# Top-k attention with a feed-forward block: small operations moved to ScalarE, and scores, value products, exponentials and sends placed elsewhere in the step

## The chip, the cores and the metric

The kernel runs on one core of one Trainium2 chip. The core has five engines that run side by side, each through its own instructions in the order in which they were written: PE (TensorE, matrix products), DVE (VectorE), ACT (ScalarE), POOL (GpSimd) and SP (SyncE, which here only issues DMAs). The metric is the device time of one execution in microseconds, as the median of several runs.

## The reference

Eight batches, eight heads, 576 positions, head width 64. Of each row of scores only the 32 largest take part in the softmax; the result feeds a layer norm, a hidden layer and a residual. The weights arrive as float64.

```python
scores = scale * np.matmul(q, k.transpose(0, 1, 3, 2))
kth = np.partition(scores, -32, axis=-1)[..., -32:-31]
scores = np.where(scores >= kth, scores, -1e9)
attn = np.exp(scores - scores.max(-1, keepdims=True))
attn = attn / (attn.sum(-1, keepdims=True) + 1e-9)
x = heads_to_columns(attn @ v)                      # (8, 576, 512)
xn = (x - mean(x)) / sqrt(var(x) + 1e-6) * g_ln
return x + maximum(xn @ w_ch1, 0) @ w_ch2           # 512 -> 2048 -> 512
```

## The kernel before

**Tiles.** Two heads form a pair. The 576 query rows of a pair are cut into four tiles of 128 rows and a rest of 64; a Unit is one such tile for both heads, so its scores are two tiles of 128 x 576. The rest units take the 64 rows of both heads as one tile. There are 160 units. Units are joined in Groups (the two or three query tiles of one Job, which is a batch and a pair), and a group's value products are made at once.

**What a unit goes through.** `scores` (L365) makes the scores on PE and copies them from PSUM with ACT (L371). `halve` (L399) splits a row on DVE into the larger and the smaller of two halves (L411, L412). `select` (L414), called four times, finds eight maxima each time and strikes them out, all on DVE (L425, L433, L419); the last one yields the 32nd value, `thr`, and the first one the maximum, `top`. `prepare` (L441) turns the maximum into the bias of the exponential with one tiny operation, on DVE in the first steps (below `CONVERTING`) and on POOL afterwards (L446). `watch` (L448) notes on DVE whether a second candidate of the smaller half could have been missed (L452). `mask` (L478, ACT) makes a steep ramp around the 32nd value, after one tiny multiplication (L482) for its bias; `lower` (L487, POOL, L488) subtracts the scores from it; `weigh` (L490, ACT, L496) takes the exponential and its sum. `move` (L519) transposes blocks of 32 x 32 on DVE (L524) from `e` into the unit's own score tile; SP then sends that tile to HBM (`send`, L540) and brings it back turned (`bring`, L532, four DMAs) as `pt`. Units that are not moved, the rest ones above all, are turned on PE instead (`turn`, L545). `values` (L606) multiplies `pt` with v on PE into `av`; `take_values` (L624) copies `av` to `oT` with ACT (L626); `place` (L636) turns `oT` on PE, and ACT writes it, divided by the sum, into the rows `x` (L630).

**The rows.** A Block is a pair of row tiles whose heads are all there. `stats` (L675) makes the mean and variance on DVE (L681, L682) and takes the mean off the rows with two POOL operations (L687, L690). `turn_x` turns the rows on PE (L715), then follow the hidden products (L756) and the projections (L913), which take seven eighths of the usual products through sums made on POOL (L843 to L849). This MLP work stands in a list, `todo`.

**The order.** Everything is written out by hand in one loop over steps (L1183). Step n runs `halve` and `select` of unit n, makes the scores of unit n + 1, masks unit n - 1 (`mk`), and weighs and moves unit n - 2 (`ex`); a group's value products come four steps behind its last unit. The step has eight calls of `fill` (L263), the slots. Each slot advances a clock (`tick`), runs what has become old enough (the classes `Later`: sends after `SEND_AGE` slots, brings `BRING_AGE` slots later), and puts as much MLP work on PE as `slot` (L1145) has planned for the step. So PE's list holds scores, value products, turns and MLP work in a fixed order, and ACT's list holds the copies that serve them between the masks and exponentials. While n is below `CONVERTING` (17), the float64 weights are also converted. `END` is the number of steps; the step at which a block's rows are taken is written at L1053. The second `compute` call (L1354) runs only if the watch finds a doubtful row.

The beginning of a step reads:

```python
for x in due(n):
    scores(x)
if g:
    values(g)
if u:
    halve(u)
    select(u, 0)
...
if ex and not early:
    weigh(ex, 0)
fill()
if ex and len(ex.tiles) > 1 and not early:
    weigh(ex, 1)
if g:
    take_values(g)
fill()
```

Of the kernel before, what the change touches and what calls it, by code (L numbers as in the profile page):

```python
# [9 lines left out]
AF = mybir.ActivationFunctionType  # L10
ALU = mybir.AluOpType
FP32 = mybir.dt.float32
# [7 lines left out]
STEEP = 2.0**90  # L20
# [9 lines left out]
def compute(  # L30
# [12 lines left out]
    nc = tc.nc  # L43
    P = nc.NUM_PARTITIONS
# [7 lines left out]
    scale = 1.0 / float(D) ** 0.5  # L52
# [9 lines left out]
    HALF = S // 2  # L62
# [123 lines left out]
    now = [-1]  # L186
# [71 lines left out]
                run()  # L258

    sums_later, ends_later, stores = Later(), Later(), Later()  # L260
    sends, brings, loads = Later(), Later(), Later()

    def fill(least=0):  # L263
        tick[0] += 1
        ends_later.settle(END_AGE)
        loads.settle(LOAD_AGE)
        brings.settle(BRING_AGE)
        sends.settle(SEND_AGE)
        fetch_forms(FETCH_AGE)
        owed[0] = min(owed[0] + share[0], 6.0)  # L270
        while todo and (not todo[0][3] or todo[0][3]()):
            if owed[0] < todo[0][1] / 2 and least <= 0:
                break
            least -= 1
            pop()
# [89 lines left out]
    def scores(u):  # L365

        u.sc = scpool.tile([P, 2, S], FP32, tag="sc", name="sc")
        made = [score_half(u, s) for s in range(2)]
        for t in range(len(u.tiles)):
            for s in range(2):  # L370
                nc.scalar.copy(  # L371
                    u.sc[:, t, s * HALF : (s + 1) * HALF], made[s][t][:, 0:HALF]
                )
# [64 lines left out]
            u.top = m  # L438
        u.thr = m

    def prepare(u):  # L441

        nt = len(u.tiles)
        u.bias, u.edge = u.thr[:, 0:nt, 5], u.thr[:, 0:nt, 6]
        eng = nc.vector if u.i < CONVERTING else nc.gpsimd
        eng.tensor_scalar(u.bias, u.top[:, 0:nt, 0], -scale, 0.0, ALU.mult, ALU.add)  # L446

    def watch(u):  # L448

        nt = len(u.tiles)  # L450
        c = 1 + 2 * (u.i % 16)
        nc.vector.tensor_tensor(  # L452
            watched[:, c : c + nt], u.hi[:, 0:nt, HALF + 7], u.thr[:, 0:nt, 7], ALU.subtract
        )
        if u.i % 16 == 15 or u.i == N - 1:
            u.ends_watch = True

    def settle_watch():

        for out, first, op in ((0, 0, ALU.max), (33, 1, ALU.min)):  # L460
# [17 lines left out]
    def mask(u, t):  # L478
        if u.e is None:
            u.e = epool.tile([P, 2, S], FP32, tag="e", name="e")  # L480
        if t == 0:
            nc.scalar.mul(u.edge, u.thr[:, 0 : len(u.tiles), 7], STEEP)  # L482
        nc.scalar.activation(  # L483
            u.e[:, t], u.sc[:, t], AF.Relu, bias=u.edge[:, t : t + 1], scale=-STEEP
        )

    def lower(u, t):  # L487
        nc.gpsimd.tensor_tensor(u.e[:, t], u.e[:, t], u.sc[:, t], ALU.subtract)  # L488

    def weigh(u, t):  # L490
        g = u.group
        if g.den is None:
            g.den = denpool.tile([P, 2 * J + 1], FP32, tag="den", name="den")
        col = 2 * u.qt + t
        u.weighed += 1
        nc.scalar.activation(  # L496
            u.e[:, t], u.e[:, t], AF.Exp, bias=u.bias[:, t : t + 1], scale=-scale,
            accum_out=g.den[:, col : col + 1],
        )
# [106 lines left out]
    def values(g):  # L606
        vb = g.job.v
        av = brief("av")
        for c in range(J):
            for h in range(2):  # L610
                nc.tensor.matmul(  # L611
                    av[h * D : (h + 1) * D, 0 : g.nq],
                    vb[:, h * J + c, :],
                    g.pt[:, 0 : g.nq // 32, 5 * h + c, :],
                    start=(c == 0),
                    stop=False,
                )
        nc.tensor.matmul(  # L618
            av[:, 0 : g.nq], g.job.ends[:], g.pt[:, 0 : g.nq // 32, J, :],
            start=False, stop=True,  # L620
        )
        g.av = av

    def take_values(g):  # L624
        g.oT = otpool.tile([P, GQ], FP32, tag="oT", name="oT")
        nc.scalar.copy(g.oT[:, 0 : g.nq], g.av[:, 0 : g.nq])  # L626
# [38 lines left out]
    class Block:  # L665
# [9 lines left out]
        def stats(self, i):  # L675
            x = self.x[i]
            if self.mv is None:
                self.mv = small.tile([P, J, 2], FP32, tag="mv", name="mv")
                self.rstd = small.tile([P, J], FP32, tag="rstd", name="rstd")
            st = brief_small.tile([P, 6], FP32, tag="st", name="st")  # L680
            nc.vector.bn_stats(out=st[:], in_=x)  # L681
            nc.vector.bn_aggr(out=self.mv[:, i, :], in_=st[:])  # L682
            if now[0] <= gives_first:
                nc.vector.tensor_scalar_sub(x, x, self.mv[:, i, 0:1])
            else:
                less = brief_small.tile([P, 1], FP32, tag="less", name="less")
                nc.gpsimd.tensor_scalar(  # L687
                    less[:], self.mv[:, i, 0:1], -1.0, 0.0, ALU.mult, ALU.add
                )
                nc.gpsimd.tensor_scalar(x, x, 1.0, less[:], ALU.mult, ALU.add)  # L690
            self.step[i] = now[0]

        def centred(self, i):
# [246 lines left out]

    PER_ROW = 1.71e-3
    SUM_AGE, END_AGE, FETCH_AGE, STORE_AGE = 7, 6, 10, 8
    SEND_AGE, BRING_AGE, LOAD_AGE = 2, 4, 4
    blocks = []
    plain_done, formed, used, fetched = [None], [None], [], [0]

# [65 lines left out]
    units = []  # L1012
# [5 lines left out]
            g.last = len(units) - 1  # L1018
        j.last = len(units) - 1
    N = len(units)  # L1020
    END = N + 7

    fresh = []
    for j in jobs:
# [25 lines left out]
    for j in jobs:  # L1050
        if j.hp == NHP - 1:
            b = j.b
            step = j.last + (3 if j.last < EARLY else 4 + units[j.last].moved)  # L1053
            tiles = [(b, qt) for g in j.groups for qt in g.qts if qt < J]
            dsts = [[(out[b, t[1] * P : (t[1] + 1) * P, :], full)] for t in tiles]
            if jobs.index(j) == NHP - 1:
                step -= 1
                j.groups[0].quick = True
            if tiles:
                add_block(step, tiles, dsts)  # L1060
            if J in j.groups[0].qts and b % 4 == 3:
# [17 lines left out]
    def at(i):  # L1079
        return units[i] if 0 <= i < N else None  # L1080
# [14 lines left out]
    def due(n):  # L1095

        return [units[n + 1]] if 0 < n < N - 1 else []
# [83 lines left out]
    for n in range(END):  # L1183
# [16 lines left out]
        last = ex and ex is ex.group.units[-1]  # L1200
        quick = ex.group if last and ex.group.quick else None

        for x in due(n):
            scores(x)
        if g:
            values(g)
        if u:
            halve(u)
            select(u, 0)
# [15 lines left out]
                weigh(ex, t)  # L1225
        if not quick:
            weights(n, 0)
        if ex and not early:
            weigh(ex, 0)
        fill()  # L1230
        if ex and len(ex.tiles) > 1 and not early:
            weigh(ex, 1)
        if g:
            take_values(g)
        fill()
        if parts:
            parts[0]()
        if ex and ex.rest:
# [6 lines left out]
        sums_later.settle(SUM_AGE)  # L1245
        for den in recips.pop(n, []):
            nc.vector.reciprocal(den, den)
        if doubt is not None and at(n - 1) and at(n - 1).ends_watch:
            settle_watch()
            if n == N:  # L1250
                tell()
        if n in turns:
            turn_heads(turns[n])
# [5 lines left out]
        fill()  # L1259
        if mk and not early:  # L1260
            mask(mk, 0)
        if g:
            place(g)
        if late:
            place_rest(late.job.b, late.job.hp)
        fill(1 if g or late else 0)
        if mk and len(mk.tiles) > 1 and not early:
            mask(mk, 1)
        fill()
        if mk and not early:  # L1270
            lower(mk, 0)
        if len(parts) > 2:
            parts[1]()
        if moved:
# [14 lines left out]
        fill()  # L1289
        if parts:  # L1290
            parts[-1]()
        if mk and len(mk.tiles) > 1 and not early:
            lower(mk, 1)
        fill()
        for x in (u if n < EARLY else None, mk if n > EARLY else None):
            if x and x is units[x.job.last]:
                load_values(x.job)
# [8 lines left out]
            weights(n, 1)  # L1306
        if u:
            select(u, 3)
            prepare(u)
        for x in (g, quick):  # L1310
            if x and x.job.hp == NHP - 1:
                for qt in x.qts:
# [73 lines left out]
```

## Time and profile before

| | us |
|---|---|
| median of three runs | 1741.08 (1738.31 to 1741.73) |
| the profiled execution | 1737.59 |
| its span, first to last instruction | 1735.7 |

| engine | busy us | share of the span |
|---|---|---|
| PE | 1485.2 | 86% |
| PE weight loads (beside the products) | 1110.8 | 64% |
| DVE | 1467.9 | 85% |
| ACT | 1032.2 | 59% |
| POOL | 1051.8 | 61% |

The 16 DMA engines move 275.19 MB, at a mean of 159 GB/s. The chain of work that ended last runs for 41% of the span on PE, 30% on DVE, 8% on ACT, 8% on DMAs and 7% on POOL. A busy share is a mean over stages with different limits; a wait is put down to what came last before the waiting instruction started. In the lines of the profile "out<-in" are the program's tile names, L is the line of the kernel, and the numbers after the bar are the group's busy time in us and the mean of one instruction in ns.

### The profile page before, as it was taken

The numbers are of one execution on the slowest core, as the hardware profiler recorded it, in microseconds if no ns is written. First come the engines' busy times: TensorE is split into PE (matmuls) and PEld (weight loads), VectorE is DVE, ScalarE is ACT, GpSimd is POOL, SyncE is SP. The second block draws the span as 40 slices with busy tenths as digits, with TensorE's granted clock in tenths as the row PEclk, the third lists the DMA queues.
The fourth block names the chain that finished last, engine by engine and source line by source line (L and its number), as shares of the span: only waits on it lengthen the run. The fifth ranks groups of instructions, "written<-read, shape, count | busy, mean of one in ns | idle before, by whom it ended". The sixth has DMA issues, their size and how long they took to land.

```text
span 1735.7 us, 26165 instructions
## 1 busy us (share of the span) xinstructions
PE 1485.2 (86%) x7412; PEld 1110.8 (64%) x7412; DVE 1467.9 (85%) x4090; ACT 1032.2 (59%) x2662; POOL 1051.8 (61%) x1321
## 2 busy tenths in 40 slices
PE   2558887887788888788899989999899899989997
PEld 1336455655566665566677766776677676768886
DVE  6979999989898998889998998899989998984100
ACT  6777765755566564556566756676566665644411
POOL 4668868646556564556656766576656665746334
PEclk9768898988999898899999999999999999989999
DMA  7525657744565465545775586556755676453411
GB/s 190 134 66 181 200 123 216 226 140 136 151 182 151 145 187 154 152 144 153 212 181 159 161 221 161 175 167 181 199 172 150 168 214 181 139 141 110 124 45 51
DMA packets 392068, 275.19 MB, mean 159 GB/s; under 512 B 254436, under 2 KB 358376, under 8 KB 391912
## 3 DMA queue, kind: packets, MB, share of 16 engines
q1 hardware_dynamic: 387176, 272.81, 55.8%
q8 instruction: 62, 1.02, 0.3%
q10 hardware_dynamic: 4736, 0.59, 0.2%
q14 instruction: 94, 0.77, 0.1%
HBM read 177.47 MB, written 95.81 MB: 157 GB/s over the span
## 4 chain that ended last, share of the span: by engine, by line
PE 41%; DVE 30%; ACT 8%; DMA 8%; POOL 7%; SPq 3%; issue 2%; DVEq 0%; ACTq 0%; POOLq 0%
PE ops L913 14%; PE hps L756 12%; DVE m L433 9%; DVE hi L419 7%; PE av L611 6%; DVE sc L524 5%; PE scps L390 4%; DMA pt<-turned 3%; POOL e L488 3%; DVE lo L412 3%; ACT e L496 2%; DVE hi L411 2%; DVE hi L425 2%; PE av L618 2%; SPq L532 2%
## 5 line engine op out<-in xcount | busy, mean ns | idle before, releaser
L488 POOL TENSOR_TENSOR e<-e,sc 128x576 f32<-128x576 f32 x288 | 424.0, 1482 | 295.8 <-ACT e L483 292.5
L756 PE MATMUL hps<-xT,w 128*128 128x256 f32 x2304 | 533.4, 384 | 3.2 <-ACT xT L718 3.2
L756 PEld LDWEIGHTS hps<-xT,w 128*128 128x128 f32 x2304 | 432.1, 192 | 74.3 <-issue 12.3
L433 DVE MAX8 m<-hi 128x8 f32<-128x296 f32 (+1 forms) x1152 | 469.9, 442 | 1.1
L419 DVE MATCH_REPLACE8 hi<-m,hi 128x288 f32<-128x288 f32 (+1 forms) x864 | 377.1, 441 | 0.0
L913 PE MATMUL ops<-w,h 128*128 128x256 f32 x1360 | 321.3, 385 | 0.0
L371 ACT COPY sc<-scps 128x288 f32<-128x288 f32 x576 | 202.7, 406 | 190.1 <-PE scps L390 167.2
L913 PEld LDWEIGHTS ops<-w,h 128*128 128x128 f32 x1360 | 256.2, 193 | 42.1 <-issue 7.5
L611 PE MATMUL av<-pt,vb 128*64 128x256 f32 (+2 forms) x1088 | 175.6, 473 | 101.4 <-DMA pt<-turned 62.7
L496 ACT ACTIVATE e<-e,m 128x576 f32<-128x576 f32 x288 | 224.9, 787 | 60.2 <-POOL e L488 59.9
L524 DVE STREAM_TRANSPOSE sc<-e 128x1152 f32<-128x1152 f32 x118 | 160.2, 1358 | 109.5 <-ACT e L496 103.0
L483 ACT ACTIVATE e<-sc,m 128x576 f32<-128x576 f32 x288 | 217.5, 774 | 5.2
L611 PEld LDWEIGHTS av<-pt,vb 128*64 128x64 f32 x1088 | 91.3, 161 | 174.4 <-issue 94.9
L446 POOL TENSOR_SCALAR m<-m 128x2 f32<-128x2 f32 (+1 forms) x143 | 109.3, 764 | 135.1 <-DVE m L433 132.0
L779 ACT ACTIVATE h<-hps 128x512 f32<-128x512 f32 x144 | 85.4, 594 | 102.3 <-PE hps L756 101.9
L412 DVE TENSOR_TENSOR lo<-sc 128x576 f32<-128x576 f32 (+1 forms) x160 | 144.2, 901 | 0.0
L390 PE MATMUL scps<-kT,qT 64*128 64x288 f32 x512 | 96.8, 480 | 46.0 <-DVE qT L320 40.6
L411 DVE TENSOR_TENSOR hi<-sc 128x576 f32<-128x576 f32 (+1 forms) x160 | 124.9, 780 | 6.6 <-ACT sc L371 6.4
L913 PE MATMUL ops<-wt,s 128*128 128x256 f32 x544 | 128.0, 383 | 0.0
L390 PE MATMUL scps<-kT,late_qT 64*128 64x288 f32 (+3 forms) x832 | 122.2, 412 | 2.1 <-ACT pt L565 2.1
L425 DVE MAX8 hi<-lo 128x8 f32<-128x288 f32 x288 | 117.8, 443 | 0.0
L913 PEld LDWEIGHTS ops<-wt,s 128*128 128x128 f32 x544 | 102.0, 192 | 16.6 <-issue 2.1
(104 smaller groups left out, 1664.4 us busy)
## 6 DMA issues: line engine op xcount, KB each, us to landing
turned<-sc SPq DMA_DIRECT2D x118, 576.0 KB, 3.3
pt<-turned SPq DMA_DIRECT2D x472, 144.0 KB, 3.0
w<-forms SPq DMA_DIRECT2D x136, 256.0 KB, 4.1
vb<-in_v_dram SPq DMA_DIRECT2D x136, 128.0 KB, 3.3
raw<-in_moe_w_ch_dram SPq DMA_DIRECT2D x32, 512.0 KB, 4.5
kT<-kept SPq DMA_DIRECT2D x36, 288.0 KB, 3.4
kin<-in_k_dram SPq DMA_DIRECT2D x128, 72.0 KB, 2.4
kept<-kT SPq DMA_DIRECT2D x32, 288.0 KB, 2.6
```

The lines of the kernel that those rows point to most:

```text
L371: nc.scalar.copy(u.sc[:, t, s * HALF : (s + 1) * HALF], made[s][t][:, 0:HALF])
L390: nc.tensor.matmul(ps[i * R : i * R + ql, o : o + width], qT[r, q0 : q0 + ql], kT[r, k0 : k0 + width], start=True, stop=True,)
L412: nc.vector.tensor_tensor(lo, a, b, ALU.min)
L419: nc.vector.match_replace(x, m[:, t, :], x, LOWEST)
L433: nc.vector.max(m[:, t, :], u.hi[:, t, 0:width])
L483: nc.scalar.activation(u.e[:, t], u.sc[:, t], AF.Relu, bias=u.edge[:, t : t + 1], scale=-STEEP)
L488: nc.gpsimd.tensor_tensor(u.e[:, t], u.e[:, t], u.sc[:, t], ALU.subtract)
L496: nc.scalar.activation(u.e[:, t], u.e[:, t], AF.Exp, bias=u.bias[:, t : t + 1], scale=-scale, accum_out=g.den[:, col : col + 1],)
L524: nc.vector.transpose(blocks.rearrange("p (j c n) -> p j c n", j=ni, n=32), u.e[:].rearrange("p t n -> p (t n)").rearrange("p (c j k) -> p ...
L611: nc.tensor.matmul(av[h * D : (h + 1) * D, 0 : g.nq], vb[:, h * J + c, :], g.pt[:, 0 : g.nq // 32, 5 * h + c, :], start=(c == 0), stop=False,)
L756: nc.tensor.matmul(ps[0][:, side * N : (side + 1) * N], w1[:, c, f * P : (f + 1) * P], self.xT[:, c, 0:N], start=(c == 0), stop=(c == NC - 1),
L913: nc.tensor.matmul(bank[name][:, 0:Q], a(j), rhs, start=first and j == 0, stop=(j == G - 1), skip_group_check=not first,)
```

## The change

It has these parts. The bias of the exponential is made by ACT in `mask`, between the masks of the unit's two tiles, and `prepare` is gone. `watch` uses, per tile, one operation with one tensor and a per-row number in place of one operation with two tensors for both tiles. Taking the mean off the rows goes from two POOL operations to two ACT operations, which are written two slots after the statistics (`CENTRE_AGE`). From step `CONVERTING` on, scores and value products are written behind the second slot, `take_values` behind the fifth and `place` at the end of the step, before the last slots. The exponential of a unit's first tile is written at the end of the step that masks it; the second stays after the first slot of the next step, which is now ahead of the scores. Sends wait four slots instead of two. Rows of a block that ends with a moved unit are taken one step later, the watch is settled one step later, and the loop has one more step.

```diff
+        centres.settle(CENTRE_AGE)
         brings.settle(BRING_AGE)
...
-    def prepare(u):
-        nt = len(u.tiles)
-        u.bias, u.edge = u.thr[:, 0:nt, 5], u.thr[:, 0:nt, 6]
-        eng = nc.vector if u.i < CONVERTING else nc.gpsimd
-        eng.tensor_scalar(u.bias, u.top[:, 0:nt, 0], -scale, 0.0, ALU.mult, ALU.add)
-    def watch(u):
-        nt = len(u.tiles)
-        c = 1 + 2 * (u.i % 16)
-        nc.vector.tensor_tensor(
-            watched[:, c : c + nt], u.hi[:, 0:nt, HALF + 7], u.thr[:, 0:nt, 7], ALU.subtract
-        )
...
         nc.scalar.activation(
             u.e[:, t], u.sc[:, t], AF.Relu, bias=u.edge[:, t : t + 1], scale=-STEEP
         )
+        if t == 0:
+            nc.scalar.mul(u.bias, u.top[:, 0:nt, 0], -scale)
+    def watch(u):
+        for t in range(len(u.tiles)):
+            c = 1 + 2 * (u.i % 16) + t
+            nc.vector.tensor_scalar(
+                watched[:, c : c + 1], u.hi[:, t, HALF + 7 : HALF + 8],
+                u.thr[:, t, 7:8], None, ALU.subtract,
+            )
...
-                less = brief_small.tile([P, 1], FP32, tag="less", name="less")
-                nc.gpsimd.tensor_scalar(
-                    less[:], self.mv[:, i, 0:1], -1.0, 0.0, ALU.mult, ALU.add
-                )
-                nc.gpsimd.tensor_scalar(x, x, 1.0, less[:], ALU.mult, ALU.add)
+                def centre():
+                    less = brief_small.tile([P, 1], FP32, tag="less", name="less")
+                    nc.scalar.mul(less[:], self.mv[:, i, 0:1], -1.0)
+                    nc.scalar.activation(x, x, AF.Identity, bias=less[:])
+                    self.step[i] = now[0]
+                centres.add(centre)
+                return
...
-    SEND_AGE, BRING_AGE, LOAD_AGE = 2, 4, 4
+    SEND_AGE, BRING_AGE, LOAD_AGE, CENTRE_AGE = 4, 4, 4, 2
...
-    END = N + 7
+    END = N + 8
...
-            step = j.last + (3 if j.last < EARLY else 4 + units[j.last].moved)
+            step = j.last + (3 if j.last < EARLY else 4 + 2 * units[j.last].moved)
...
-        for x in due(n):
-            scores(x)
-        if g:
-            values(g)
+        first = n < CONVERTING
+        if first:
+            for x in due(n):
+                scores(x)
+            if g:
+                values(g)
...
-        if ex and not early:
-            weigh(ex, 0)
         fill()
         if ex and len(ex.tiles) > 1 and not early:
             weigh(ex, 1)
-        if g:
+        if g and first:
             take_values(g)
         fill()
+        if not first:
+            for x in due(n):
+                scores(x)
+            if g:
+                values(g)
...
-        if g:
+        if g and first:
             place(g)
-        if late:
+        if late and first:
             place_rest(late.job.b, late.job.hp)
-        fill(1 if g or late else 0)
+        fill(1 if first and (g or late) else 0)
...
         if mk and not early:
             lower(mk, 0)
+        if g and not first:
+            take_values(g)
...
-        if mk and len(mk.tiles) > 1 and not early:
-            lower(mk, 1)
-        fill()
+        if mk and not early:
+            if len(mk.tiles) > 1:
+                lower(mk, 1)
+            weigh(mk, 0)
+        if not first:
+            if g:
+                place(g)
+            if late:
+                place_rest(late.job.b, late.job.hp)
+        fill(1 if not first and (g or late) else 0)
...
         if u:
             select(u, 3)
-            prepare(u)
```

More of the change, by code (lines that the diff above doesn't have):

```diff
@@ L260, in compute @@
     sums_later, ends_later, stores = Later(), Later(), Later()
-    sends, brings, loads = Later(), Later(), Later()
+    sends, brings, loads, centres = Later(), Later(), Later(), Later()
     def fill(least=0):
@@ L439, in select @@
         u.thr = m
-    def prepare(u):
-        nt = len(u.tiles)
-        u.bias, u.edge = u.thr[:, 0:nt, 5], u.thr[:, 0:nt, 6]
-        eng = nc.vector if u.i < CONVERTING else nc.gpsimd
-        eng.tensor_scalar(u.bias, u.top[:, 0:nt, 0], -scale, 0.0, ALU.mult, ALU.add)
-    def watch(u):
-        nt = len(u.tiles)
-        c = 1 + 2 * (u.i % 16)
-        nc.vector.tensor_tensor(
-            watched[:, c : c + nt], u.hi[:, 0:nt, HALF + 7], u.thr[:, 0:nt, 7], ALU.subtract
-        )
-        if u.i % 16 == 15 or u.i == N - 1:
-            u.ends_watch = True
     def settle_watch():
@@ L480, in mask @@
             u.e = epool.tile([P, 2, S], FP32, tag="e", name="e")
+        nt = len(u.tiles)
         if t == 0:
-            nc.scalar.mul(u.edge, u.thr[:, 0 : len(u.tiles), 7], STEEP)
+            u.bias, u.edge = u.thr[:, 0:nt, 5], u.thr[:, 0:nt, 6]
+            nc.scalar.mul(u.edge, u.thr[:, 0:nt, 7], STEEP)
         nc.scalar.activation(
@@ L485, in mask @@
         )
+        if t == 0:
[7 more added lines that the diff above has]
+            )
+        u.ends_watch = u.i % 16 == 15 or u.i == N - 1
     def lower(u, t):
@@ L1247, in compute @@
             nc.vector.reciprocal(den, den)
-        if doubt is not None and at(n - 1) and at(n - 1).ends_watch:
+        if doubt is not None and at(n - 2) and at(n - 2).ends_watch:
             settle_watch()
-            if n == N:
+            if n == N + 1:
                 tell()
```

## The prediction

> **What bounds the kernel now.** I read the utilisation row, then the windows by stage, then the list of waits, then one episode in the timeline. The windows give, per stretch: length, busy time of PE, PEld, DVE, ACT, POOL, then TensorE clock, DMA share and GB/s.
>
> ```profile
> 174.00:434.00 260.00, 210.34 (x1035) 140.51 (x1034) 248.93 (x679) 161.60 (x425) 178.13 (x192) 0.88 0.62 173
> 434.00:694.00 260.00, 219.46 (x1108) 162.72 (x1107) 238.00 (x659) 154.72 (x416) 146.79 (x186) 0.93 0.58 162
> 694.00:954.00 260.00, 229.14 (x1181) 173.45 (x1179) 237.47 (x665) 155.52 (x414) 157.45 (x210) 0.95 0.59 167
> 954.00:1214.00 260.00, 244.73 (x1270) 186.84 (x1272) 248.67 (x722) 168.34 (x445) 165.42 (x213) 0.97 0.64 178
> 1214.00:1474.00 260.00, 239.48 (x1251) 183.21 (x1247) 243.14 (x691) 160.90 (x425) 160.39 (x212) 0.97 0.64 180
> 1474.00:1600.00 126.00, 117.63 (x580) 93.25 (x579) 102.09 (x284) 68.98 (x180) 76.83 (x108) 0.96 0.46 135
> 1600.00:1736.00 136.00, 123.82 (x609) 106.14 (x607) 9.28 (x24) 34.45 (x79) 55.77 (x101) 0.97 0.24 72
> ```
>
> From 174 to 1600 us DVE is busy 1318.3 of 1426 us, idle 107.7. The last 136 us are PE's alone. So the middle is worth what DVE's idle time and DVE's work there are worth. The waits (us in total, times, longest) name that idle time:
>
> ```profile
> ACT sc L371 <- PE scps L390: 167.2, 132, 5.4
> ...
> ACT oT L626 <- PE av L618: 108.2, 37, 11.8
> DVE sc L524 <- ACT e L496: 103.0, 34, 9.3
> ...
> PE av L611 <- DMA pt<-turned: 62.7, 19, 9.5
> ```
>
> Nearly all of DVE's idle time is one wait: the transposition in move (L524) waits for the exponential (L496). The timeline shows how one arises (start, duration, engine, line; in brackets the idle time before it and what ended that):
>
> ```profile
> 718.46 0.43 ACT L626 COPY oT<-av 128x320 f32<-128x320 f32 x1 [11.83 <-PE av L618]
> ...
> 719.02 0.77 ACT L483 ACTIVATE e<-sc,m 128x576 f32<-128x576 f32 x1
> ...
> 724.54 1.49 ACT L371 COPY sc<-scps 128x288 f32<-128x288 f32 x4 [2.01 <-PE scps L390]
> ...
> 725.90 0.80 ACT L496 ACTIVATE e<-e,m 128x576 f32<-128x576 f32 x1
> ...
> 726.67 0.78 ACT L496 ACTIVATE e<-e,m 128x576 f32<-128x576 f32 x1
> ...
> 727.57 1.38 DVE L524 STREAM_TRANSPOSE sc<-e 128x1152 f32<-128x1152 f32 x1 [7.88 <-ACT e L496]
> ```
>
> The reader is to see two queueing accidents, not work. ACT stood 11.83 us at the copy of the value products with the mask behind it; then it stood 2.01 us at the score copies with both exponentials behind them. ACT itself is 59% busy.
>
> Is PE full too? It is busy 94% at 954 to 1214, but in a stretch where the chain of waits runs on PE without a gap (911 to 933) the scores start at 917.8, 925.3 and 932.9: 7.5 us a step without value products. Those take 3.1 us in two steps of five (16 and 2 matmuls, 2.3 and 0.7 to 0.8 us), so PE needs about 8.7 us a step. The mean distance between two L411 (halve) from step 20 on is 9.7 us. DVE's need in its fullest window is 248.7/260 x 9.7 = 9.3 us. DVE is the bound, PE a close second.
>
> **What the Trainium skill says.** "Perfetto Trace Analysis", Per-engine timelines, Tensor Engine Instruction: ACT, DVE and GpSimd are strict first-in first-out. The episode agrees: exponentials whose input was ready stood behind copies. "Trainium Kernel Development and Optimization", Performance Expectations: matmul busy time is a bad metric as matmuls are pipelined; 94% busy against 8.7 of 9.7 us agrees. "SBUF — State Buffer", Who interferes with whom: a DVE instruction with two SBUF inputs, or in a two-port mode, fully blocks against a GpSimd one that reads SBUF; with one input outside those modes it does not. The trace agrees for two inputs: the 128x2 subtraction of watch has a median of 230 ns, a mean of 436, a maximum of 1397.
>
> **The change part by part.**
>
> *Watch.*
>
> ```profile
> L452 DVE TENSOR_TENSOR watched<-hi,m 128x2 f32<-128x2 f32 (+1 forms) x160 | 69.7, 436 | 0.0
> L446 POOL TENSOR_SCALAR m<-m 128x2 f32<-128x2 f32 (+1 forms) x143 | 109.3, 764 | 135.1 <-DVE m L433 132.0
> ```
>
> 160 two-input operations become 288 one-input ones (128 units of two tiles, 32 of one). No 128x1 operation with a pointer stands in the main part; the nearest are L470 and L471, 154 and 143 ns. At 150 ns: 43.2, gain 69.7 - 43.2 = 26.5 us. If it takes the port after all, the nearest row is L446 on DVE (17 operations, mean 284 ns): 81.8, loss 12. I take -26.
>
> *Bias on ScalarE.* POOL loses 109.3 us, DVE 17 x 0.284 = 4.8 us in the start. ACT gains 160 x 0.207 (L482, the same operation and shape) = 33 us between the two masks. It delays the second mask by 0.2 us, which has a whole step until move; cost 0. POOL's 132 us of waiting at L446 were idle anyway. But L446 fires at the end of select 3, just where halve's two-input operations begin. Means of 780 and 901 ns against medians of 739 and 750 make some 50 us of excess in L411 and L412; how much is L446's the trace doesn't say. Between -25 and +10 (POOL's other operations may land there), I take -5.
>
> *Centring on ScalarE, two slots later.* POOL loses 26.8 + 3.8 + 7.6 = 38 us. ACT gains 34 x (0.2 + 0.71) = 31 us; 0.71 is an estimate from "ScalarE: Activation LUTs", What ACT_TABLE_LOAD costs (280 ns with a pointer bias, 0.833 ns per element); with the second pointer it gives 0.80, and L734 measures 0.805. ACT goes from 1032 to 1096 us. A wait for DVE's statistics now stands on ACT (L687 had 25.8 us in 13). Until the next slot's products nothing urgent is behind it; PE's wait at L715 for POOL's centring (27.3 us) shrinks. Cost 0, ends -10 and +15.
>
> *First exponential at the end of the step, second ahead of the scores.* They no longer stand behind the score copies and the four copies' 1.5 us; masks no longer stand behind the value copy, which goes to the fifth slot. What is left ahead of the first exponential is the subtraction on POOL (L488, 1.4 us) and the value copy. With values starting at slot 2 (2.4 us at 9.7/8 = 1.2 us a slot), scores 1.2, products 3.1, copy 0.4, exponential 1.0, the exponentials stand at about 9 us into the step, and move wants them some 6 us into the next, at about 16. PE may be 7 us late; now it is 6 less 1.2 for the score matmuls, 1.0 for the rest of the copies and 2.0 for both exponentials: 1.8. Queued behind the exponential's wait on POOL are place's copies and the next score copies. Rest units gain too: PE's 86 us at L553 for their exponentials (49.3 PEld, 36.8 PE, partly the same time).
>
> *Scores and value products behind the second slot.* They come 2.4 us later. Measured over steps 14 to 158 in the timeline, the score matmuls start in the median 0.7 us before the halve of their step, and 4.1 us after it in one of ten; from their end to the halve that needs them there are 8.7 us in the median, 5.3 at the fifth percentile. Less 2.4, less 1.0 for the last copy, less 1.0 for an exponential ahead: 4.3 and 0.9 left. Few new waits: +7 us (ends 0 and +140, below). place ends the step; the row statistics of the 32 tiles want it some 6 us later: +5 (0 to +30).
>
> *Sends two slots later* (118 sends, 472 brings on SP, 0.33 us and about 0.45 us each). The bring moves from slot 3 to slot 5, the products from slot 0 to slot 2: five slots between, as before, for 3.0 us of landing. SP stood 404 us at sends for DVE, so fewer loads queue behind one; but the sends pass more loads, forms and head copies. 0, from -20 to +30.
>
> *Block one step later, one more closing step.* In the lists of instructions 366 MLP matmuls follow the last scores instead of 369, of 2168: -1 us. The tail of 136 us stays.
>
> **Sum.** Of the 107.7 us of DVE's idle time I let three quarters go (81), since the largest waits all have the two accidents: -81 + 7 + 5 - 26 - 5 - 1 = -101. DVE then needs 9.1 us a step and PE 8.7; where products bunch PE gives some back: 20 to 25 us. Net -78 on the profiled execution's 1737.6 us: 1660; the median of the runs, 1741.1, lies 3.5 above it: 1663.
>
> **The rivals.** *PE takes over* (0.20): DVE's wait turns into waits for scores and rows on bunched steps; half the idle time stays. For: PE chain 41% of the span. Against: the gapless stretch. 9.7 to 9.45 us over 147 steps: -37, 1704. *The re-timing does nothing* (0.07): the first exponential waits for POOL's subtraction as long as before; 59.9 us of such waits exist. Only watch pays: 1714. *Scores come too late* (0.13), the slower one: place L411. Margins of 0.9, 2.4, 4.3 and 6.9 us (5th, 25th, 50th and 75th percentile) are eaten if PE's lateness grows. At 4 us more a step waits 0.95 us on average, 147 x 0.95 = 140 us, less the 101: 1780. It decides from about 3.5 us on.
>
> **How the numbers follow.** The likeliest (0.60) is 1663, alone 1630 to 1700. With the two smaller gains, and the unknown costs, 1625 to 1738 leaves out the slower case and a little of the low end. A difference of 0.2% is about what this measurement can tell from none; faster 0.85, within 0.03, slower 0.12.
>
> **What would show it.** Right: L524's wait for e under 30 us; watch rows near 150 ns with no long tail; DVE over 96% busy in the middle; ACT's wait for av under 40 us; the same closing 136 us. Wrong: more than 40 us at L411 behind score copies, DVE's idle time as before with POOL as releaser of the exponential, or watch above 240 ns.

## The result, and the profile after

The changed kernel takes 1722.84 us (median of four runs, 1722.36 to 1727.08) against 1741.40: a ratio of 0.9902, 95% interval 0.9882 to 0.9922. That is 19 us less where 78 were forecast. The profiled execution, the longest of the four, took 1727.08 us (span 1725.2) against 1737.59.

The waits (engine, line, what it waited for: us in total, times, longest) are the first place to look, since the forecast lived on one of them:

```profile
ACT e L495 <- POOL e L487: 127.5, 134, 6.3
ACT h L782 <- PE hps L759: 120.6, 57, 10.0
...
DVE sc L523 <- ACT e L495: 91.2, 32, 13.6
ACT o L881 <- PE ops L916: 82.4, 27, 10.5
ACT sc L372 <- PE scps L391: 74.5, 86, 5.1
ACT oT L625 <- PE av L617: 50.2, 16, 7.2
ACT t L890 <- PE ops L916: 50.1, 27, 5.5
```

In the kernel before, ACT's waits for the products of the MLP were:

```profile
ACT h L779 <- PE hps L756: 101.9, 68, 6.0
...
ACT t L887 <- PE ops L913: 61.2, 29, 8.2
...
ACT o L878 <- PE ops L913: 56.8, 37, 5.6
```

The two queueing accidents did shrink: ACT's waits for score and value products fell from 167.2 + 108.2 to 74.5 + 50.2 us. But ACT's waits for the MLP's products (h, o and t) rose from 219.9 (101.9 + 56.8 + 61.2) to 253.1, and DVE's wait for the exponential only fell from 103.0 to 91.2.

The groups of instructions (out<-in, count, busy us, mean ns of one, idle time before them and its releasers):

```profile
L610 PE MATMUL av<-pt,vb 128*64 128x256 f32 (+2 forms) x1088 | 177.2, 478 | 106.7 <-DMA pt<-turned 42.3 <-DMA vb<-in_v_dram 17.8 <-DMA out_dram<-o 10.9
...
L523 DVE STREAM_TRANSPOSE sc<-e 128x1152 f32<-128x1152 f32 x118 | 160.2, 1358 | 99.6 <-ACT e L495 91.2 <-POOL s L846 8.4
L413 DVE TENSOR_TENSOR lo<-sc 128x576 f32<-128x576 f32 (+1 forms) x160 | 145.4, 909 | 0.0
L412 DVE TENSOR_TENSOR hi<-sc 128x576 f32<-128x576 f32 (+1 forms) x160 | 143.1, 894 | 16.9 <-ACT sc L372 16.8
...
L480 DVE TENSOR_SCALAR watched<-hi,m 128x1 f32<-128x1 f32 x288 | 47.7, 201 | 0.0
```

The same groups in the kernel before (watch stands in the prediction):

```profile
L611 PE MATMUL av<-pt,vb 128*64 128x256 f32 (+2 forms) x1088 | 175.6, 473 | 101.4 <-DMA pt<-turned 62.7 <-DMA w<-forms 11.0 <-ACT den L508 7.9
...
L524 DVE STREAM_TRANSPOSE sc<-e 128x1152 f32<-128x1152 f32 x118 | 160.2, 1358 | 109.5 <-ACT e L496 103.0 <-POOL s L843 6.3
...
L412 DVE TENSOR_TENSOR lo<-sc 128x576 f32<-128x576 f32 (+1 forms) x160 | 144.2, 901 | 0.0
...
L411 DVE TENSOR_TENSOR hi<-sc 128x576 f32<-128x576 f32 (+1 forms) x160 | 124.9, 780 | 6.6 <-ACT sc L371 6.4
```

The reader is to see three things. PE still stands over 100 us ahead of the value products (101.4 before). halve's two operations take 288.5 us instead of 269.1. And watch fell from 69.7 to 47.7 us; its shortest and longest instruction are 194 and 214 ns (142 and 1397 before), so its long tail is gone.

To place the loss I took each halve in the timeline as the start of a step and compared the two kernels by steps, with DVE's idle time inside them:

| steps | before, us | idle | after, us | idle |
|---|---|---|---|---|
| 0 to 10 | 131.6 | 22.2 | 130.0 | 27.1 |
| 10 to 30 | 200.7 | 6.9 | 217.4 | 27.6 |
| 30 to 80 | 488.8 | 42.1 | 449.9 | 15.2 |
| 80 to 120 | 372.3 | 19.5 | 383.6 | 19.8 |
| 120 to 159 | 388.6 | 40.0 | 389.7 | 34.9 |

In steps 30 to 80 the forecast came true: two thirds of the idle time went, and 39 us with it. Steps 10 to 30 gave 17 us back: in them DVE's wait for the exponential rose from 6.0 to 17.1 us, and 8.0 us of waits for score copies are new. Steps 80 to 120 gave another 11 back without any more idle time: there halve's two operations take 73.9 us instead of 62.2. The last steps gained nothing. The end of the span after the last halve is 142 us before and 143 after.

What a wait in the later steps now looks like (timeline: start, duration, engine, line; in brackets the idle time before and its releaser):

```profile
1052.63 1.75 SPq L531 DMA_DIRECT2D pt<-turned  x4
...
1057.26 4.07 PE L610 MATMUL av<-pt,vb 128*64 128x320 f32 x16 [3.41 <-DMA pt<-turned]
...
1062.96 0.60 ACT L782 ACTIVATE h<-hps 128x512 f32<-128x512 f32 x1 [7.00 <-PE hps L759]
1063.45 0.20 ACT L468 ACTIVATE m<-m 128x2 f32<-128x2 f32 x1
...
1064.54 2.77 POOL L487 TENSOR_TENSOR e<-e,sc 128x576 f32<-128x576 f32 x2 [9.39 <-ACT e L469]
...
1068.93 1.38 DVE L523 STREAM_TRANSPOSE sc<-e 128x1152 f32<-128x1152 f32 x1 [4.55 <-ACT e L495]
```

PE stands for `pt`, which SP asked for 4.6 us earlier. The MLP products written behind the value products come late, ACT stands 7.00 us at their copy, and masks, subtractions, exponentials and DVE's transposition follow. The value copy is no longer first in ACT's list; another copy of a PE product has its place.

My theory after this: the wait begins with the **late transfer** of `pt`, and moving ACT's instructions only changes which copy passes it on. Its rivals: **the port** (halve's operations, which read two tensors, collide with POOL's reads), **the blocked DMA queue** (the later send keeps SP free) and **the early exponential** (ACT now stands at POOL's subtraction).

### The profile page after: what moved, and what is told of

It reads as the page before. It is cut to its first block, busy times and chain, and to the rows that moved or that the text cites. A ratio compares the mean times of both kernels' runs of the same rounds, so it can differ in the third digit from the quotient of the medians.

```text
span 1725.2 us, 26539 instructions
## 1 busy us (share of the span) xinstructions
PE 1476.9 (86%) x7412; PEld 1105.6 (64%) x7412; DVE 1462.3 (85%) x4201; ACT 1077.4 (62%) x2890; POOL 935.8 (54%) x1110
## 5 line engine op out<-in xcount | busy, mean ns | idle before, releaser
L759 PEld LDWEIGHTS hps<-xT,w 128*128 128x128 f32 x2304 | 433.8, 192 | 77.4 <-issue 17.1
L916 PE MATMUL ops<-w,h 128*128 128x256 f32 x1360 | 317.8, 382 | 0.0
L495 ACT ACTIVATE e<-e,m 128x576 f32<-128x576 f32 x288 | 224.0, 778 | 128.7 <-POOL e L487 127.5
L610 PE MATMUL av<-pt,vb 128*64 128x256 f32 (+2 forms) x1088 | 177.2, 478 | 106.7 <-DMA pt<-turned 42.3
L372 ACT COPY sc<-scps 128x288 f32<-128x288 f32 x576 | 198.9, 407 | 104.3 <-PE scps L391 74.5
L523 DVE STREAM_TRANSPOSE sc<-e 128x1152 f32<-128x1152 f32 x118 | 160.2, 1358 | 99.6 <-ACT e L495 91.2
L469 ACT ACTIVATE e<-sc,m 128x576 f32<-128x576 f32 x288 | 221.8, 770 | 5.2
L610 PEld LDWEIGHTS av<-pt,vb 128*64 128x64 f32 x1088 | 90.1, 163 | 180.9 <-issue 109.5
L412 DVE TENSOR_TENSOR hi<-sc 128x576 f32<-128x576 f32 (+1 forms) x160 | 143.1, 894 | 16.9 <-ACT sc L372 16.8
L413 DVE TENSOR_TENSOR lo<-sc 128x576 f32<-128x576 f32 (+1 forms) x160 | 145.4, 909 | 0.0
L916 PEld LDWEIGHTS ops<-wt,s 128*128 128x128 f32 x544 | 102.4, 192 | 16.8 <-POOL h L852 1.5
L391 PEld LDWEIGHTS scps<-kT,late_qT 64*128 64x128 f32 (+1 forms) x832 | 69.8, 169 | 54.6 <-issue 25.8
```

The costliest lines, as they stand in the source:

```text
L372: nc.scalar.copy(u.sc[:, t, s * HALF : (s + 1) * HALF], made[s][t][:, 0:HALF])
L391: nc.tensor.matmul(ps[i * R : i * R + ql, o : o + width], qT[r, q0 : q0 + ql], kT[r, k0 : k0 + width], start=True, stop=True,)
L413: nc.vector.tensor_tensor(lo, a, b, ALU.min)
L469: nc.scalar.activation(u.e[:, t], u.sc[:, t], AF.Relu, bias=u.edge[:, t : t + 1], scale=-STEEP)
L495: nc.scalar.activation(u.e[:, t], u.e[:, t], AF.Exp, bias=u.bias[:, t : t + 1], scale=-scale, accum_out=g.den[:, col : col + 1],)
L523: nc.vector.transpose(blocks.rearrange("p (j c n) -> p j c n", j=ni, n=32), u.e[:].rearrange("p t n -> p (t n)").rearrange("p (c j k) -> p ...
```

## Experiments

Each ratio is to the kernel before on the same chip, with its 95% interval. The runs were made on several chips, so kernels are best compared by their ratios. Idle times and waits are those of one profiled execution each. The edits stand against the changed kernel unless a heading says otherwise.

### Sends after two slots again

```diff
-    SEND_AGE, BRING_AGE, LOAD_AGE, CENTRE_AGE = 4, 4, 4, 2
+    SEND_AGE, BRING_AGE, LOAD_AGE, CENTRE_AGE = 2, 4, 4, 2
```

> The changed kernel with sends after two slots again (SEND_AGE 2), all else kept. Late-transfer theory: PE stands at the value products because pt is brought late, ACT's next copy of a PE product stands with it, and DVE's transposition behind that; two slots more between send and products take PE's wait for pt (42 us) to under 20 and DVE's wait for the exponential (91 us) to under 60: 1700 to 1712 us against 1723. Port theory (the missing gain went into collisions of halve with POOL): no change, 1720 to 1726. Theory of the blocked DMA queue (the later send was needed to keep SP free): slower, 1730 or more, with SP's waits at the send back above 350 us.

Measured: 1701.48 us, ratio 0.9777 (0.9744 to 0.9809). The groups of this kernel:

```profile
L610 PE MATMUL av<-pt,vb 128*64 128x256 f32 (+2 forms) x1088 | 171.1, 465 | 76.5 <-DMA pt<-turned 32.1 <-DMA kin<-in_k_dram 9.0 <-DMA w<-forms 8.2
...
L523 DVE STREAM_TRANSPOSE sc<-e 128x1152 f32<-128x1152 f32 x118 | 160.1, 1357 | 76.2 <-ACT e L495 67.9 <-POOL s L846 8.4
```

The time is in the band of the late transfer; the two waits (32 and 68 us) fell less than I had written. PE's whole idle time ahead of the value products fell by 30 us and DVE's wait by 23. SP stands longer at the send for DVE (335.8 instead of 217.2 us) and shorter at the bring for the send's landing (149.1 instead of 265.9); the sum is the same (485 and 483 us) and the time fell, so the blocked queue falls. One other thing came with the send: the score copy into a tile that is still being sent waits for it, 14.3 us on ACT in the changed kernel and 3.2 here. This run can't tell that from the late `pt`.

### The bias back on POOL

```diff
-            nc.scalar.mul(u.bias, u.top[:, 0:nt, 0], -scale)      # in mask
+            prepare(u)                                            # behind select 3, as before
```

> The changed kernel with the bias of the exponential back on POOL (DVE in the first steps) at the end of select 3, all else kept. Port theory: POOL is again held at that small operation until select 3 ends, so its subtractions fall less on halve; L412 and L413 together go from 288 us to about 269, time 1710 to 1720. Late-transfer theory: the collisions are chance, L412 and L413 stay within 8 us of 288 and the time is the same to 8 us slower (1722 to 1731), since DVE gets 5 us more work in the start.

Measured: 1724.16 us, 0.9887 (0.9857 to 0.9917), the same as the changed kernel. L412 and L413 take 282.3 us together, 6 less, where the port, by way of the bias, asked for 19. Where the bias is made is not what puts POOL on halve.

### Scores, products and place at their old places

```diff
-        first = n < CONVERTING
+        first = True
```
(and SEND_AGE 2)

> The changed kernel with scores, value products, their copy and place at their places of the kernel before, and sends after two slots (so that five slots lie between bring and products, as in both kernels); the exponentials keep their new places. If the new places of scores and products are what made steps 30 to 80 shorter (489 to 450 us), this falls back to 1732 to 1742 us, with DVE's wait for the exponential at 90 to 110. If the early exponentials did it alone, it stays at 1718 to 1728. Steps 10 to 30 (217 us after, 201 before): if the switch of places at step 17 costs there, they go back to about 201.

Measured: 1727.38 us, 0.9923 (0.9897 to 0.9948). The time lies in the second band, at its upper end, but DVE's wait is 117.8 us, above the first one's, and ACT's wait at the value copy 142.8, longer than in the kernel before: neither expectation held as a whole.

Against the earlier sends with the new places (1701.48) the difference is 26 us, most of it in steps 30 to 80 (474.7 against 446.2 us). But this isn't the worth of the places alone, since there the products also lie seven slots behind the bring, and here five. With five slots in both (the transfer and the products both two slots later) stands the changed kernel, 1722.84 us, and the two intervals overlap: it is 25 us shorter in steps 30 to 80 (449.9) and 9 and 11 us longer in steps 10 to 30 and 80 to 120. So the new places alone gain in one stretch, and no gain over the whole is shown.

Steps 10 to 30 take 208.1 us against 208.2 with the same send and the new places, so the switch of places at step 17 doesn't show as a cost. L412 and L413 take 276.8 us, 12 less than with the new places.

### The first exponential at the start of the step

```diff
-            weigh(mk, 0)           # end of the step
+        if ex and not early:
+            weigh(ex, 0)           # start of the next
```

> The changed kernel with the first tile's exponential back at the start of the next step (behind nothing but the step's first weights; scores and products stay behind the second slot). If the early exponential does anything, it is that it no longer waits in ACT's list behind place and the last slots' copies: 3 to 12 us slower, 1726 to 1735. If it costs by making ACT stand at POOL's subtraction (127 us of such waits after, 60 before), this is 5 to 15 us faster, 1708 to 1718, and that wait is under 90 us.

Measured: 1722.14 us, 0.9894 (0.9868 to 0.9919). ACT's wait for POOL falls from 127.5 to 70.1 us and the time doesn't move: that wait lay beside other work. In this order the early exponential neither pays nor costs; neither expectation held.

### Sends after two slots, brings three slots later

```diff
-    SEND_AGE, BRING_AGE, LOAD_AGE, CENTRE_AGE = 4, 4, 4, 2
+    SEND_AGE, BRING_AGE, LOAD_AGE, CENTRE_AGE = 2, 3, 4, 2
```

> The changed kernel with sends after two slots and brings three slots after them (instead of four and four): eight slots between bring and products. Late-transfer theory: a further shortening of PE's idle time before the value products, 2 to 8 us below the 1701 us of the kernel with earlier sends. Blocked-queue theory: SP now stands at the bring until the send has landed (3.4 us), the loads and forms behind it come late, and the time rises to 1705 to 1715.

Measured: 1690.20 us, 0.9719 (0.9694 to 0.9745). One slot more is worth another 10 us by the ratios, a little more than expected; the two intervals just touch. The send is where it was, so this gain can't come from the tile that a send sets free.

```profile
L610 PE MATMUL av<-pt,vb 128*64 128x256 f32 (+2 forms) x1088 | 165.1, 452 | 69.2 <-DMA pt<-turned 14.1 <-DMA kin<-in_k_dram 10.4 <-DMA dr<-den 8.7
```

### The kernel before, sends after four slots

```diff
-    SEND_AGE, BRING_AGE, LOAD_AGE = 2, 4, 4
+    SEND_AGE, BRING_AGE, LOAD_AGE = 4, 4, 4
```

> The kernel before with only the later send (SEND_AGE 4 in place of 2): three slots between bring and products instead of five. Late-transfer theory: PE waits longer at the value products, idle time before L611 well above its 101 us, and the time rises to 1755 to 1775. Blocked-queue theory, by which a later send frees SP: 1725 to 1741, and SP's wait for DVE at the send falls from 404 to about 220 us.

Measured: 1766.80 us, 1.0166 (1.0136 to 1.0196), slower by 28 us, as the late transfer has it:

```profile
L611 PE MATMUL av<-pt,vb 128*64 128x256 f32 (+2 forms) x1088 | 186.8, 497 | 128.7 <-DMA pt<-turned 70.9 <-DMA vb<-in_v_dram 19.1 <-DMA kin<-in_k_dram 10.1
L524 DVE STREAM_TRANSPOSE sc<-e 128x1152 f32<-128x1152 f32 x118 | 160.4, 1360 | 140.2 <-ACT e L496 133.7 <-POOL s L843 6.3
```

PE waits 27 us longer ahead of the value products, and DVE 31 us longer for the exponential. ACT's score copies wait 21.0 us for the send instead of 3.4. Steps 10 to 30 take 211.7 us instead of 200.7. So the change contains a part that is harmful by itself and hid under the others.

### Value products behind the fourth slot

```diff
-            values(g)              # behind slot 2
-            take_values(g)         # behind slot 5
+            values(g)              # behind slot 4
+            take_values(g)         # directly ahead of place
```

> The changed kernel, sends after four slots as it has them, but the value products written behind the fourth slot instead of the second and their copy directly ahead of place. Seven slots between bring and products, gained at the other end than with earlier sends. Late-transfer theory: the same cure by other means, 1698 to 1712 us, DVE's wait for the exponential below 75 us. If it is the early send itself that helps (the unit's own score tile freed sooner, or another order in SP's list), no gain: 1718 to 1728.

Measured: 1730.51 us, 0.9956 (0.9934 to 0.9978): slower even than the changed kernel (0.9882 to 0.9922), a miss for the theory as I had put it. PE's idle time at L610 did fall to 75.6 us, as far as with the earlier sends, and DVE's idle time in steps 30 to 120 from 35.0 to 18.4 us. But steps 10 to 30 took 227.2 us instead of 217.4, with 15.2 us of waits for scores in them, and L412 and L413 took 292.2. Less standing of PE is not enough, then: bought at this end, it costs elsewhere what it brings. Why it costs so much in the start I didn't test.

No gain is what the rival in the text above expects, that the early send helps by something else than the slots. That can't be the whole, since the earlier bring gained with the send left alone; how much of the send's 21 us belongs to it stays open.

### Masks ahead of the scores, alone and with earlier sends

```diff
         if not first:
+            if mk:
+                for t in range(len(mk.tiles)):
+                    mask(mk, t)
             for x in due(n):
                 scores(x)
```
(the masks at slots 3 and 5 only while `first`)

> The changed kernel with sends after two slots, and both masks written ahead of the scores (behind the second slot) from step 17 on. Queue-head theory: what is left of DVE's wait (68 us) is masks that stand in ACT's list behind copies of PE's products; with the masks ahead the wait falls to 30 to 45 us and the time to 1675 to 1695. If by now DVE's own work and the closing PE stretch set the time, or the masks, coming earlier, only put POOL's subtractions on halve (L412 and L413 above 290 us), it stays at 1698 to 1708.

> The changed kernel, sends after four slots as it has them, with only both masks written ahead of the scores from step 17 on. If two separate things hold the gain back, the late transfer and the masks that stand behind the score copies and so push POOL's subtractions onto the next halve, this alone gives about what it gave on top of the earlier send (22 us): 1698 to 1706 us, L412 and L413 together at about 266 us instead of 288. If the masks only help once the transfers are early, 1712 to 1722.

Measured: with earlier sends 1678.92 us, 0.9656 (0.9629 to 0.9684); alone 1704.83 us, 0.9798 (0.9767 to 0.9829). Both times are as expected. With earlier sends the reason is not: DVE's wait for the exponential stays at 66.9 us (84.5 alone). What went is the collisions, as expected for the masks alone. The groups with earlier sends, then alone:

```profile
L412 DVE TENSOR_TENSOR hi<-sc 128x576 f32<-128x576 f32 (+1 forms) x160 | 134.4, 840 | 14.3 <-ACT sc L372 13.9
L413 DVE TENSOR_TENSOR lo<-sc 128x576 f32<-128x576 f32 (+1 forms) x160 | 131.6, 822 | 0.0
```

```profile
L412 DVE TENSOR_TENSOR hi<-sc 128x576 f32<-128x576 f32 (+1 forms) x160 | 137.7, 861 | 18.0 <-ACT sc L372 17.6
L413 DVE TENSOR_TENSOR lo<-sc 128x576 f32<-128x576 f32 (+1 forms) x160 | 134.2, 838 | 0.0
```

266.0 and 271.9 us instead of 289.3 and 288.5. For each lengthened operation of halve I looked for the POOL instruction that was under way when it began; the lengthened one ends about 0.6 us after that one does. POOL's subtractions hold 34 us of the lengthening before, 47 after, 13 and 18 with the masks ahead, and 27 with scores and products at their old places. Scores written behind the second slot put four copies ahead of the masks, so masks and subtractions drift towards the next halve: of the 140 halves from step 20 on, 27 begin under a subtraction in the kernel before, 51 in the changed one, 18 and 24 with the masks ahead. There DVE pays. That is the port, but through the masks, not through the bias.

### The kernel before with the one-input note only

```diff
-        nc.vector.tensor_tensor(watched[:, c : c + nt], u.hi[...], u.thr[...], ALU.subtract)
+        nc.vector.tensor_scalar(watched[:, c : c + 1], u.hi[...], u.thr[:, t, 7:8], None, ALU.subtract)
```

> The kernel before with only the note by one-input operations (watch of the changed kernel). The prediction's value for it was 26 us less of DVE's work: if DVE sets the pace of the middle, 1715 to 1725 against 1740; if the time saved on DVE is lost to its wait for the exponential, 1733 to 1741, with that wait up by 10 us or more.

Measured: 1734.42 us, 0.9965 (0.9949 to 0.9981).

```profile
L524 DVE STREAM_TRANSPOSE sc<-e 128x1152 f32<-128x1152 f32 x118 | 160.7, 1362 | 121.6 <-ACT e L496 115.5 <-POOL s L843 6.2
...
L452 DVE TENSOR_SCALAR watched<-hi,m 128x1 f32<-128x1 f32 x288 | 48.0, 203 | 0.0
```

DVE does 21.7 us less, and 12.5 of it come back as a longer wait for the exponential (103.0 to 115.5). In time the saving is worth 5 to 6 us. Work taken from DVE is not worth its duration while DVE waits for something that keeps its own time.

### All three, and the old start

Sends after two, brings after three, masks ahead of the scores; the second one also keeps the first exponential at its old place while weights are converted.

```diff
+        if ex and not early and n <= CONVERTING:
+            weigh(ex, 0)
...
-            weigh(mk, 0)
+            if not first:
+                weigh(mk, 0)
```
(the second one's own part)

> The changed kernel with sends after two slots, brings three slots later, and masks ahead of the scores. If the three act on different waits, their gains add: 1701 - 11 - 22, 1665 to 1672 us. If the closing PE stretch and DVE's work are what is left, 1673 to 1680.

> As the one with all three, but below step 17, while the weights are converted, the first tile's exponential stays at the start of the next step as in the kernel before. If the exponential's wait for POOL, which is full of conversions there, is what makes steps 10 to 30 longer (217 us after, 201 before, 204 to 208 with earlier sends), these steps go to about 198 and the time falls by 4 to 8 us; if it is the switch of the places at step 17, nothing changes.

Measured: 1676.12 us, 0.9629 (0.9597 to 0.9660), and 1670.64 us, 0.9588 (0.9558 to 0.9619). Bring and mask gains don't add fully (1665 to 1672 was the sum). The second is 5.5 us shorter in the median, as far as was expected, and the single times hardly overlap (1671.51 to 1680.90, and 1664.87 to 1671.60). But steps 10 to 30 take 202.9 and 201.7 us, so the gain isn't where it was expected, and the two profiled executions (1671.65 and 1670.99) don't show it elsewhere. With the kernel before at 200.7 there was little left to win here, so this pair can't say what made these steps 217 us long. What is left is seen in the windows (length; busy PE, PEld, DVE, ACT, POOL; clock, DMA share, GB/s) of the second one:

```profile
694.00:954.00 260.00, 250.15 (x1309) 192.18 (x1307) 256.28 (x755) 179.13 (x499) 150.33 (x190) 0.98 0.63 176
954.00:1214.00 260.00, 245.80 (x1303) 189.36 (x1302) 255.53 (x756) 172.55 (x489) 137.89 (x179) 0.99 0.70 193
```

DVE is busy 98% in the middle, 237.5 and 248.7 of 260 us in the kernel before. This is the state that the prediction had expected of the change itself, with a gain of 70 us. From step 20 on a halve follows the last one after 9.2 us in the mean (9.7 in the kernel before, 9.6 in the changed one). From the last halve to the end of the span it is now 151 us, against 142: PE falls behind a little once DVE is quick.

## Why the prediction was wrong

*Direction and range.* Faster was right; 1722.84 lies in the range, 60 us off the likeliest value. The direction owes little to the mechanism: of the sum's three large terms, -81 became -11, -26 became -22, and -5 became +19. In the profile DVE's work is nearly what it was (1467.9 and 1462.3 us). The change's parts turned out as follows.

*Watch.* The mechanism was right (no tail). An operation takes 201 ns, not 150, so the row fell by 22 us, not 26; what the path gets of it alone is about 5 to 6 us (ratio 0.9965). The step that failed here: taking DVE's saved work at its full duration.

*First exponential and value products.* This is the step that failed most: "of the 107.7 us of DVE's idle time I let three quarters go (81), since the largest waits all have the two accidents." In the profile, steps 10 to 159 lost 11 us of DVE's idle time. I took the place at which ACT stood for the cause. A cause lies ahead of it: PE's standing ahead of the value products (101.4 us, 62.7 of them for `pt`, the fourth line of waits in the prediction, and not followed). While PE stands there, all that is written behind it is late, and ACT stands at whichever copy comes next: in the episodes shown, the value copy before and the hidden layer's afterwards. Moving the transfer shows it in both kernels: three to five slots between bring and products (the kernel before) 28 us, five to seven (the changed one) 21, seven to eight another 10. Moving the products back instead, also to seven slots, shortened PE's standing as much and gained nothing, so the slots are not the whole account.

*Sends.* Zero, "five slots between, as before", was consistent for the waits (101.4 and 106.7 us), but "as before" was the trouble: those five slots were the largest thing left to gain. Undone, the later send is worth 21 us; in the kernel before it costs 28 by itself, just inside the end of +30.

*Bias and port.* The value was -5 with +10 as the upper end; halve's two operations took 19.4 us more. The bias is innocent (6 us). The trace of before could have said so: of the 50 us of excess 34 come with the subtractions (L488), and none with L446. The scores' new place pushed masks and subtractions towards halve; with the masks ahead, 17 to 23 us go, with scores and products at their old places 12. I had costed what the moved scores wait for, and not where the instructions behind them on ACT, and then on POOL, would land.

*Start.* That steps 10 to 30 would lose 17 us was in no step. The later send alone costs them 11 in the kernel before. With earlier sends the changed kernel loses 7 there, with scores and products at their old places besides 7 also, with masks ahead and brings earlier 2. So a good part of it is the send; the rest stays open. The first exponential back at its old place in all steps takes 4 off, one profile against another, which may be chance.

*What held.* Waits at halve for score copies grew from 6.4 to 16.8 us, where +7 was forecast. DVE's need of 9.1 us a step was nearly right: the last kernels come to 9.2. Centring takes 0.72 us an operation on ACT (0.71 forecast), and no cost of it or of the bias is visible; but PE's wait for the centred rows, which was to shrink from 27.3 us, is 28.8, and centring was not run by itself. The closing stretch stayed at 142 to 143 us. PE as a close second bound shows only in the last kernels.

*The rivals.* The nearest in time was the second, by which the re-timing does nothing (1714). Its reason is not the right one: 57 us of ACT's wait for POOL's subtraction could go with the time unchanged. And the watch, which alone was to pay 26 us there, pays 5 to 6.

The Trainium skill's sentence on strict first-in first-out order ("Perfetto Trace Analysis", Per-engine timelines) agrees with the episodes shown: ACT stood 7.00 us at the hidden layer's copy, and the mask behind it started only then. I read it as a reason to move instructions, where the next question was what the head of the list waits for, and what that one waits for in turn.

## What to carry to other kernels

Follow a wait back until an engine stands for something that isn't another engine's list, here a transfer; moving what stood behind it can only choose the next victim. When instructions are moved on one in-order engine, look where those behind them land on every engine further on, above all on operations that share a port. Test a bundle's parts one by one: here one constant was worth as much, undone (21 us), as the whole bundle gained (19 us).

## What the runs showed of the hardware

Value products that had waited ran slower as well. Sixteen passes at 320 columns took 2.38 us in the kernel before at 908 us, where PE had stood 0.42 us; they took 4.07 us at 1057 us in the changed one, after 3.41 us of standing. The clock that the profile shows as granted to PE was 1.00 in the first stretch and 0.58 in the second, and 2.38 / 0.58 is 4.1: the clock accounts for the whole difference.

The other groups of this kind in these two profiles agree. There are 56. All 34 that began after less than 2 us of standing took 2.37 to 2.38 us at a clock of 1.00. Of the seven after 2.0 to 2.8 us, four did the same and three took 3.5 to 4.1 us. All 15 after more than 2.8 us took 3.3 to 4.5 us, at clocks of 0.50 to 0.69. In these profiles a late transfer was so paid twice. That the standing itself lowers the clock is read from these groups; no run tested it. Over whole kernels the mean of a pass goes with the idle time ahead only roughly: from 452 ns at 69.2 us to 497 at 128.7, but also 455 at 75.6 and 483 at 104.0.

halve shows the shared port. Where a POOL operation was under way as it began, it ended about 0.6 us after that operation did: in the changed kernel a halve operation began at 1323.72 us, the subtraction ended at 1324.71, the halve operation at 1325.32. That one took 1.60 us; the shortest of its kind took 0.73.
